# A spectral mixer with an MLP, forward and backward: order and engines in the opening stage

## The chip, the cores and the metric

The kernel runs on one core of a Trainium2 chip, in one launch. The metric is the device time of a run in microseconds (us). The core's engines, as the profile names them: PE (TensorE, matrix products; PEld are its weight loads), DVE (VectorE), ACT (ScalarE), POOL (GpSimd) and SP (SyncE, which only issues transfers here). Each works through its own instruction list in order and waits on semaphores for the others. Transfers are issued from SP's queue and from POOL's, and run on the same 16 DMA engines.

## The reference

The program computes a forward pass and all its gradients, for x of 2048 positions and 448 channels (S = 2048, D = 448), in bfloat16:

```
h  = x + irfft2(rfft2(layernorm(x)) * (w_r + i w_i))        # 2048 x 225 spectral weights
h2 = h + mlp(layernorm(layernorm(h)))                       # over positions: w1 2048x1792, gelu, w2 1792x2048
out, vjp = jax.vjp(h2, x, w_r, w_i, w1, b1, w2, b2);  grads = vjp(grad_out)
```

There are eight outputs: h2 and the gradients of the seven inputs. The gradient before the gelu needs w2 transposed times grad_out, which depends on no other stage: it is used as filler.

## The kernel before

Everything stays in SBUF where it can. Positions are cut into 16 rows h of 128 partitions. The stages, in order of time:

1. **Opening.** x comes in four quarters of four rows (`ld_x`). `Norm.stats` (L712) makes the statistics of a row on DVE (L717, L719); after the fourth row of a quarter `close` (L723) computes the root on ACT (L727) and the factors `rn` on DVE (L730, L732), and `make` (L774) or, for the first quarter, `make_mirrored` (L757) writes the *normal forms* `xln`: x scaled and shifted, on ACT (L777) or DVE (L780), whichever the planner picks from `self.alts`.
2. **Row transform** (`fft_rows`, L791). The first quarter goes straight to PE. For the others DVE *folds* the forms (two `u`, four `w`, L806, and a small copy, L525); then PE multiplies `w` with the table `kf`, and the result is copied from PSUM to `zt`.
3. **Column transform** (`fft_cols`, L830): PE products with `df` and, after additions on DVE (`gg`, L853), with `hf`, giving the spectrum `xs`. It starts when all of `zt` is there.
4. **Spectral product** (`cmul`, L887): DVE multiplies `xs` with the weights `w_t` (`t_r` and `t_i`, L896; results written into `w_t`, L903 and L905), in five groups of columns. The first `t_r` reads the weights as a whole, so it waits for all of `w_t`.
5. **Inverse transform** (`ifft_cols`, `ifft_rows`): products with `hi`, `di0`, `kinv`; DVE makes `eo` (L977, L979) and h (L1064), then statistics, and POOL writes the normal forms `hln` of h.
6. **Filler.** w2 transposed times grad_out (`ps_mg<-go_n,w2T`): 14 blocks of 16 products. A block needs its turned weights `w2T[j]`. Blocks 0 and 1 are loaded plain and turned on PE (`turn`, L603: 16 products with the identity in two halves, each copied out of PSUM by ACT or DVE, L612); the others are loaded by transposing transfers, which occupy SP's queue while they are set up.
7. **First layer** (`ps_mp<-hln,w1c`), gelu and its derivative on ACT and DVE (L1128 to L1148), second layer (`ps_mp<-gT,w2c`), and the backward stages: `ps_mm<-du,w1T` with the layernorm's gradient (`norm_back`), the transforms again, and the weight gradients.

**What sets the order.** The kernel only records operations (`Plan.op`): which engines can do each, with estimated costs, what it reads and writes, and a priority level `pl.boost`. `Plan.order` (L257) then places them one by one: the engine and the operation that can start first by the estimates; of those that can start at the same time, the one with the highest level plus remaining path. The result is a fixed instruction list for each engine. So a changed cost, level or alternative moves instructions on all engines. Transfers on SP have a fixed sequence, that of their `ld` calls (`place`); in the planner one server with a rate in bytes per us stands for the DMA engines.

**What the change touches.** The loads of the spectral weights, `ld_w` (L622): four transfers of 450 KB, for the real and the imaginary part, each in a lower half (partitions 0 to 63) and an upper half, all on SP, between the turned blocks w2T(3) and w2T(4). The normal forms in `Norm.make` (L774). The turning of the two plain blocks of w2 (L1030) and the loop over x's quarters (L1039), where `pl.boost` is 60 for the first quarter's statistics and 0 for the others.

Of the kernel before, what the change touches and what calls it, by code (L numbers as in the profile page):

```python
# [18 lines left out]
P = 128  # L19
S = 2048  # L20
D = 448
DF = 225
# [3 lines left out]
NJ = 16  # L26
# [395 lines left out]
def kernel(  # L422
# [40 lines left out]
    pl = Plan(nc, tc, rings)  # L463

    def const(name, shape, dtype=BF16):
        ring(name, 1)
        return pl.buf(name, shape, name, dtype)
# [10 lines left out]
    def big(i, shape, name, dtype=BF16):  # L478
        return pl.buf(f"X{i}", shape, name, dtype)
# [85 lines left out]
    x = big(0, [P, NT, D], "x")  # L565
# [37 lines left out]
    def turn(j, w2n):  # L603
        for a in range(0, NT, 8):
            pt = bank(sp[0], [P, 8, P], BF16)

            def go(e, on, a=a, pt=pt):
                for t in range(8):
                    e.transpose(pt[:, t], w2n[:, (a + t) * P:(a + t + 1) * P], ident[:])

            pl.op(mm(*[128] * 8), go, r=[(w2n, a), ident], w=[pt])
            copy(on_act(1024) + [("DVE", 0.62, 0.70)], lambda a=a: w2T[j][:, a:a + 8, :], lambda pt=pt: pt[:], [pt], [(w2T[j], a)])  # L612
            turned.append(pl.ops[-1])
# [5 lines left out]
        ld(t, lambda b: b[:], hnd[name].ap(), int(np.prod(shape)) * 2)  # L619
        return t  # L620

    def ld_w(dst):  # L622
        for c, src in enumerate((A_w_r, A_w_i)):
            v = src.rearrange("(q b r) k -> b q r k", b=2, r=NJ)
            for b_ in range(2):
                ld_parts(dst, [(c, b_)], lambda b, c=c, b_=b_: b[64 * b_:64 * b_ + 64, c], v[b_], 64 * NJ * DF * 2,
                         rate=0.225)

    ld_x(0)
    kf = const("kf", [P, 5, P])  # L630
# [13 lines left out]
    ld_w2T(2)  # L644
    ld_w2T(3)
    w_t = big(4, [P, 2, NJ, DF], "w_t")
    ld_w(w_t)
    ld_w2T(4)
    kinv = table("kinv", "kinv", [P, 3, P])
    di0 = table("di0", "di", [P, 2, 2, DC])  # L650
# [14 lines left out]
    def ld_w1(slot, j0, j1):  # L665
# [3 lines left out]
        for a in range(j0, j1, 2):  # L669
# [12 lines left out]
          w=[warm])  # L682
# [20 lines left out]
    class Norm:  # L703
# [6 lines left out]
        alts = [("DVE", 0.305, 0.39), ("ACT", 0.65, 0.76)]  # L710
# [63 lines left out]
        def make(self, dst, h):  # L774
            def go(e, on):
                if on == "ACT":
                    e.activation(out=dst[:, h, 0:D], in_=self.src[:, h, :], func=ACT.Identity,  # L777
                                 scale=self.rn[:, h, 0:1], bias=self.rn[:, h, 1:2])
                else:
                    e.tensor_scalar(out=dst[:, h, 0:D], in0=self.src[:, h, :], scalar1=self.rn[:, h, 0:1],  # L780
                                    scalar2=self.rn[:, h, 1:2], op0=ALU.mult, op1=ALU.add)

            pl.op(self.alts, go, r=[(self.src, h), (self.rn, (h, 0)), (self.rn, (h, 1))], w=[(dst, h)])

        def factors(self):

# [241 lines left out]

    xln = big(1, [P, NT, 450], "xln")
    for j in w2n:  # L1030
        turn(j, w2n[j])
    pl.boost = 60.0
    for k, sign in ((1, 1.0), (2, -1.0), (3, -1.0), (4, 1.0)):
        pl.op(on_act(128), lambda e, on, k=k, sign=sign: e.activation(
            out=kf[:, k, :], in_=kf[:, 0, :], func=ACT.Copy, scale=sign), r=[(kf, 0)], w=[(kf, k)])
# [2 lines left out]
    zt = big(2, [DC, 4, 32, 64], "zt")  # L1038
    for g in range(4):  # L1039
        for h in range(4 * g, 4 * g + 4):  # L1040
            pl.boost = 60.0 if g == 0 else 0.0
            nx.stats(h)
        pl.boost = 0.0
        if g == 0:
            for o in turned[:2]:
                o.soft.add(nx.root.idx)
        fft_rows(xln, zt, g, g == 0)
    xs = big(3, [P, 2, NJ, DF], "xs")
    fft_cols(zt, df1, xs)
    negate(hi, lambda: hi[:, :, 0, :], lambda: hi[:, :, 2, :], 1024, [(hi, 0)], [(hi, 1)])  # L1050
# [9 lines left out]
    for h in range(NT):  # L1060
        with grouped():
# [3 lines left out]
                out=hn[:, h, :], in0=py[:], in1=hn[:, h, :], scale=1.0, scalar=0.0, op0=ALU.add, op1=ALU.add,  # L1065
# [16 lines left out]
    for src, dst, n in ((b1r, b1c, NFB), (b2r, b2c, NT)):  # L1082
        pb = bank("mg", [P, n], BF16)
        pl.op(mm(128), lambda e, on, pb=pb, src=src, n=n: e.transpose(pb[:], src[:], ident[0:n, 0:n]),
              r=[src, ident], w=[pb])
        copy([("DVE", 0.1, 0.2)], lambda dst=dst: dst[:], lambda pb=pb: pb[:], [pb], [dst])
    pl.op(small(), lambda e, on: e.tensor_scalar(out=b1q[:], in0=b1c[:], scalar1=Q6, scalar2=None, op0=ALU.mult),
          r=[b1c], w=[b1q])
# [27 lines left out]
    for j in range(NFB):  # L1116
# [7 lines left out]
        def gop(alts, r, w, fn, ge=ge):  # L1124
# [4 lines left out]
            out=g(uf), in_=pu[:, 0:D], func=ACT.Identity, bias=b1c[:, j:j + 1]))  # L1129
        gop([("ACT", 0.516, 0.62)], [pu, b1q], [q_], lambda e, g, j=j, pu=pu: e.activation(  # L1130
            out=g(q_), in_=pu[:, 0:D], func=ACT.Square, bias=b1q[:, j:j + 1], scale=Q6))
# [88 lines left out]
    for t in range(NT):  # L1220
# [5 lines left out]
            r=[p2, b2c, hr[t // 2]], w=[h2])  # L1226
# [254 lines left out]
```

## Time and profile before

| what | value |
|---|---|
| three runs | 335.44, 336.0, 336.9 us; median 336.0 |
| the profiled execution | 335.88 us; its span 334.1 us; mean granted clock of TensorE 0.995 |
| transfers | 81.01 MB, mean 242 GB/s over the span |
| spectral weights w_t from SP (before the first spectral product) | two of w_r and two of w_i, 450 KB each |

How to read it: the span goes from the first to the last instruction; the run's time also holds what lies around it. A timeline row gives the start, the length, the engine, the line and operation, output and inputs, how many instructions the row merges, and in brackets how long the engine was idle before and what ended that. A row of the windows view gives the stretch, its length, the busy time and the count of PE, PEld, DVE, ACT and POOL, then PE's granted clock, the share of the DMA engines and GB/s. A row of the transfers' list gives destination and source, the queue, how many, KB of each and the median time from issue to landing. Matmuls are pipelined and their ends are modelled, so rows of PE overlap by a little.

### The profile page before, as it was taken

Reading aid. Unit: us, or ns where it says so; the run is one execution under the profiler, and the core shown is the slowest. Engines: PE = TensorE matmul, PEld = TensorE weight load, DVE = VectorE, ACT = ScalarE, POOL = GpSimd, SP = SyncE. Lnnn points to the kernel's source line nnn. Section 1 sums busy time; section 2 is a strip of 40 time slices with the busy share of each in tenths; the row PEclk is TensorE's granted clock in tenths of the full one; section 3 lists DMA queues with packets and bytes.
Section 4 is the critical chain, followed back from the end, with each engine's and each line's share of the span. In section 5 each row is a group of like instructions: output and inputs, shape, how many; then the busy total and the mean of one; then the engine's idle time right before and its main releaser. Section 6 shows DMA issues by size and latency. Waiting matters only on the chain.

```text
span 334.1 us, 7003 instructions
## 1 busy us (share of the span) xinstructions
PE 323.8 (97%) x2554; PEld 176.2 (53%) x2554; DVE 267.7 (80%) x762; ACT 207.1 (62%) x459; POOL 56.3 (17%) x98
## 2 busy tenths in 40 slices
PE   8969999999999999999999999999999999999994
PEld 2547755666655555555555555555555554454441
DVE  5997999898839999062157887797989799999994
ACT  3886744376668766082302222398887788988883
POOL 0000000036440111040232000000001114455100
PEclk9979999999999999999999999999999999999999
DMA  7999899998699999999989999999995326766656
GB/s 243 379 225 230 176 211 229 239 238 242 203 325 275 334 336 253 304 272 359 260 190 228 244 215 219 240 252 186 259 269 218 125 112 231 272 205 232 237 211 221
DMA packets 136319, 81.01 MB, mean 242 GB/s; under 512 B 94396, under 2 KB 128572, under 8 KB 136156
## 3 DMA queue, kind: packets, MB, share of 16 engines
q1 hardware_dynamic: 130620, 60.45, 77.1%
q0 software_dynamic: 5664, 20.10, 16.7%
q8 instruction: 20, 0.33, 0.4%
q14 instruction: 15, 0.12, 0.1%
HBM read 30.98 MB, written 27.08 MB: 174 GB/s over the span
## 4 chain that ended last, share of the span: by engine, by line
PE 70%; DVE 23%; ACT 3%; issue 2%; DMA 1%; DVEq 0%; ACTq 0%
PE ps_mp L536 25%; PE ps_mm L536 17%; PE ps_mg L536 10%; PE ps_sp L536 6%; PE ps_sb L536 5%; DVE junk L1262 4%; DVE junk L1285 3%; DVE bs_x L717 3%; PE ps_mw L536 3%; PE ps_mm L540 2%; ACT v L1267 2%; DVE gg L853 2%; DVE u L806 1%; DVE w L806 1%; DVE go_r L1288 1%
## 5 line engine op out<-in xcount | busy, mean ns | idle before, releaser
L523 ACT CAST s<-ps_mm 128x512 bf16<-128x512 f32 (+1 forms) x108 | 56.3, 580 | 6.2 <-PE ps_mm L536 5.4
L536 PE MATMUL ps_mm<-du,w1T 128*128 128x449 bf16 x224 | 43.4, 353 | 0.0
L536 PE MATMUL ps_mp<-hln,w1c 128*128 128x448 bf16 x224 | 42.9, 352 | 0.0
L536 PE MATMUL ps_mp<-gT,w2c 128*128 128x448 bf16 x224 | 42.9, 352 | 0.0
L536 PE MATMUL ps_mm<-goT,g_t 128*128 128x512 bf16 (+1 forms) x191 | 41.0, 380 | 0.0
L536 PE MATMUL ps_mg<-go_n,w2T 128*128 128x448 bf16 x180 | 39.9, 359 | 0.0
L536 PE MATMUL ps_mm<-du_t,hlnT 128*128 128x448 bf16 (+1 forms) x208 | 39.2, 353 | 0.0
L1267 ACT ACTIVATE v<-ps_mm,nm,rn_h 128x448 f32<-128x448 f32 x16 | 11.6, 724 | 43.0 <-DVE nm L1280 43.0
L536 PEld LDWEIGHTS <-w1T 128*128 128x128 bf16 x224 | 21.7, 97 | 21.0
L536 PEld LDWEIGHTS <-w2c 128*128 128x128 bf16 x224 | 21.9, 98 | 20.5
L536 PEld LDWEIGHTS <-w1c 128*128 128x128 bf16 x224 | 21.9, 98 | 20.3
L536 PEld LDWEIGHTS <-hlnT 128*128 128x128 bf16 (+1 forms) x256 | 19.3, 97 | 21.3 <-issue 7.0
L1224 DVE SCALAR_TENSOR_TENSOR h<-ps_mp,b2c,hr 128x448 bf16<-128x448 f32 x16 | 9.8, 677 | 16.7 <-PE ps_mp L536 16.7
L536 PEld LDWEIGHTS <-w2T 128*128 128x128 bf16 x180 | 16.2, 99 | 12.7 <-issue 1.5
L536 PEld LDWEIGHTS <-g_t 128*128 128x128 bf16 (+1 forms) x191 | 13.2, 96 | 17.1 <-issue 6.0
L1132 DVE SCALAR_TENSOR_TENSOR ge<-ge 128x448 bf16<-128x448 bf16 x14 | 8.7, 621 | 13.4 <-ACT ge L1130 13.4
L1128 ACT ACTIVATE ge<-ps_mp,b1c 128x448 bf16<-128x448 f32 x14 | 8.8, 626 | 14.1 <-PE ps_mp L536 12.8
L1262 DVE CUSTOM_DVE_ANT_0 junk<-v,hln 128x448 bf16<-128x448 f32 x16 | 10.0, 623 | 7.8 <-ACT v L1267 7.7
L515 POOL DMA_DIRECT2D hn_d<-x x4 | 2.4, 588 | 75.0 <-DVE rn_h L732 71.2
L536 PEld LDWEIGHTS <-kinv 128*128 128x128 bf16 x144 | 11.3, 98 | 6.7 <-DVE eo L979 2.5
L1267 ACT ACTIVATE v<-y,nm,rn_x 128x448 f32<-128x448 f32 x16 | 12.3, 771 | 3.8 <-DVE nm L1274 3.8
L1231 ACT ACTIVATE gb2j<-go_r 128x448 bf16<-128x448 bf16 x16 | 9.2, 574 | 7.6 <-DMA go_r<-in_grad_out_dram 7.2
(157 smaller groups left out, 629.1 us busy)
## 6 DMA issues: line engine op xcount, KB each, us to landing
w2c<-in_B_w_dram SPq DMA_DIRECT2D x8, 896.0 KB, 9.1
w1c<-in_B_w_dram SPq DMA_DIRECT2D x6, 1024.0 KB, 11.2
out_dram<-s POOLq DMA_DIRECT2D x8, 512.0 KB, 3.0
out_dram<-s POOLq DMA_DIRECT2D x8, 448.0 KB, 3.4
out_dram<-s SPq DMA_DIRECT2D x7, 448.0 KB, 2.6
out_dram<-s SPq DMA_DIRECT2D x6, 512.0 KB, 5.2
x<-in_A_x_dram SPq DMA_DIRECT2D x4, 448.0 KB, 6.6
go_n<-in_grad_out_dram SPq DMA_DIRECT2D x2, 896.0 KB, 10.3
```

Source lines behind the costliest of these rows:

```text
L523: e.copy(out=out(), in_=in_())
L536: e.matmul(out, lhsT=lhsT, rhs=rhs(), start=start, stop=stop)
L540: e.matmul(out[a:b_], lhsT=lhsT[:, a // each:b_ // each], rhs=rhs(), start=start, stop=stop)
L717: pl.op(on_dve(448, 1.0e-3, 0.07), lambda e, on: e.bn_stats(out=bs[:], in_=self.src[:, h, :]), r=[(self.src, h)], w=[bs])
L806: pl.op(tt(4 * n), lambda e, on: e.tensor_tensor(out=out(), in0=in0(), in1=in1(), op=op), r=r, w=w_)
L1128: gop([("ACT", 0.516, 0.62)], [pu, b1c], [uf], lambda e, g, j=j, pu=pu: e.activation(out=g(uf), in_=pu[:, 0:D], func=ACT.Identity, bias=b1 ...
L1132: gop(stt, [q_, uf], [zz], lambda e, g: e.scalar_tensor_tensor(out=g(zz), in0=g(q_), scalar=6.0 * GELU_C, in1=g(uf), op0=ALU.add, op1=ALU. ...
L1224: pl.op([("DVE", 0.595, 0.68)], lambda e, on, t=t, p2=p2, h2=h2: e.scalar_tensor_tensor(out=h2[:], in0=p2[:, 0:D], scalar=b2c[:, t:t + 1], ...
L1231: pl.op([("ACT", 0.70, 0.80)], lambda e, on, h=h: e.activation(out=gb2j[:], in_=go_r[:, h, :], func=ACT.Copy, accum_out=gb2[:, h:h + 1]), ...
L1262: pl.op([("DVE", 0.605, 0.73)], lambda e, on: e.tensor_tensor_reduce(out=junk[:], in0=src(), in1=xhat(), scale=scale(), scalar=0.0, op0=AL ...
L1267: pl.op([("ACT", 0.53, 0.64)], lambda e, on: e.activation(out=v[:], in_=rowsum(), func=ACT.Identity, scale=nm.rn[:, h, 0:1], bias=ab[:, 1:2]),
L1285: pl.op([("DVE", 0.595, 0.68)], lambda e, on: e.scalar_tensor_tensor(out=junk[:], in0=xhat(), scalar=by(), in1=v[:], op0=ALU.mult, op1=ALU ...
```

## The change

Five edits:

- In the turning of w2's two plain blocks, the second block gets level 100.
- The statistics of x's second quarter get level 50.
- The normal forms of x's third and fourth quarters may be made by POOL too.
- The first use of `ld_w` loads only the lower halves on SP, with another rate in the planner's estimate.
- The upper halves are loaded by a new function, `ld_w_upper`, from POOL's queue. Its first operation copies one column of the last normal form (`xln` of row 15) to `mark`, and the two transfers read `mark`, so they are issued behind it.

```diff
-    def ld_w(dst):
+    def w_rows(src):
+        return src.rearrange("(q b r) k -> b q r k", b=2, r=NJ)
+
+    def ld_w_upper(dst, gate, key):
+        mark = const("mark", [P, 1])
+        pl.op([("POOL", 0.1, 0.2)], lambda e, on: e.tensor_copy(out=mark[:], in_=gate()), r=[key], w=[mark])
         for c, src in enumerate((A_w_r, A_w_i)):
-            v = src.rearrange("(q b r) k -> b q r k", b=2, r=NJ)
-            for b_ in range(2):
+            def go(e, on, c=c, src=src):
+                e.dma_start(out=dst[64:128, c], in_=w_rows(src)[1])
+            pl.op([("POOL", 0.6, 0.6)], go, r=[mark], w=[(dst, (c, 1))], dma=(64 * NJ * DF * 2, 0.335e6, False))
+
+    def ld_w(dst, halves=2):
+        for c, src in enumerate((A_w_r, A_w_i)):
+            v = w_rows(src)
+            for b_ in range(halves):
                 ld_parts(dst, [(c, b_)], lambda b, c=c, b_=b_: b[64 * b_:64 * b_ + 64, c], v[b_], 64 * NJ * DF * 2,
-                         rate=0.225)
+                         rate=0.225 if halves == 2 else 0.335)
...
-    ld_w(w_t)
+    ld_w(w_t, 1)
...
-            pl.op(self.alts, go, r=[(self.src, h), (self.rn, (h, 0)), (self.rn, (h, 1))], w=[(dst, h)])
+            alts = self.alts + [("POOL", 0.72, 0.78)] if self.nm == "x" and h // 4 in (2,3,) else self.alts
+            pl.op(alts, go, r=[(self.src, h), (self.rn, (h, 0)), (self.rn, (h, 1))], w=[(dst, h)])
...
     for j in w2n:
+        pl.boost = 100.0 if j else 0.0
         turn(j, w2n[j])
...
-            pl.boost = 60.0 if g == 0 else 0.0
+            pl.boost = (60,50,0,0)[g]
             nx.stats(h)
...
         fft_rows(xln, zt, g, g == 0)
+    ld_w_upper(w_t, lambda: xln[:, 15, 0:1], (xln, 15))
     xs = big(3, [P, 2, NJ, DF], "xs")
```

In the instruction lists of the changed program, the opening differs so:

- PE: the 16 products of block 1 stand right behind the turning of it, ahead of the fold products of x's second quarter; 50 block products, not 38, stand ahead of the first column product. The two small turns of the biases (L1084) and the fifth block come earlier among the column products.
- ACT: three normal forms behind the first quarter's, not eight, and one copy of the second turned block, not two; that copy stands behind one `du` eviction.
- DVE: three forms of the second quarter, not one, then the statistics of the third and the fourth quarter with the two `u` folds of the second between them, then the third quarter's factors, the other copy of the turned block, three forms, and the remaining folds. The first `t_r` stands behind 12 `gg` additions and one eviction, where it was 18 and two.
- POOL: three normal forms, the copy to `mark` and two transfers of `w_t`, all ahead of its work of before.
- SP: two transfers fewer, the rest in the order of before.
- From about 180 us on, the lists of all engines are the same but for a few neighbours exchanged on DVE.

## The prediction

> **What bounds the kernel now.** I read the page first (busy shares, then the clock by slices), then the timeline of TensorE, then those of the engines that end its waits.
>
> ```profile
> span 334.1 us, 7003 instructions
> ...
> PE 323.8 (97%) x2554; PEld 176.2 (53%) x2554; DVE 267.7 (80%) x762; ACT 207.1 (62%) x459; POOL 56.3 (17%) x98
> ...
> GB/s 243 379 225 230 176 211 229 239 238 242 203 325 275 334 336 253 304 272 359 260 190 228 244 215 219 240 252 186 259 269 218 125 112 231 272 205 232 237 211 221
> ```
>
> TensorE is busy for 323.8 of 334.1 us, so only 10.3 us of idle time can be had there. The profiled execution took 335.88 us, 1.8 us more than its span and 0.1 us under the median of 336.0. I make the sum against 335.88. The timeline shows where the idle time is (start, length, instructions, and in brackets the idle time before):
>
> ```profile
> 13.74 3.19 PE L536 MATMUL ps_mg<-go_n,w2T 128*128 128x448 bf16 x16
> 17.10 1.07 PE L609 MATMUL ps_sp<-ident,w2n 128*128 128x128 bf16 x16 [0.17 <-DMA w2n<-in_B_w_dram]
> 20.89 1.90 PE L536 MATMUL ps_sp<-kf,w 128*113 128x128 bf16 x16 [2.72 <-DVE w L525]
> 22.58 3.72 PE L536 MATMUL ps_mg<-go_n,w2T 128*128 128x448 bf16 x14
> ...
> 27.03 0.54 PE L536 MATMUL ps_mg<-go_n,w2T 128*128 128x448 bf16 x2
> ...
> 28.30 1.30 PE L536 MATMUL ps_mg<-go_n,w2T 128*128 128x448 bf16 x6
> 29.53 1.23 PE L536 MATMUL ps_sp<-df,zt 113*64 113x113 bf16 x40
> ```
>
> The large hole is 2.72 us, ended by VectorE's fold of x's second quarter. What follows it is slow as well:
>
> ```profile
> 20.00:22.00 2.00, 1.11 (x11) 1.11 (x12) 2.00 (x10) 2.00 (x4) 0.00 (x0) 0.75 1.39 170
> 22.00:24.00 2.00, 2.00 (x12) 1.19 (x11) 1.50 (x5) 2.00 (x5) 0.00 (x0) 0.50 1.73 228
> ```
>
> The third column from the right is the granted clock: 0.75, then 0.50. The 14 block products from 22.58 take 3.72 us, where 14/16 of the row at 13.74 are 2.79; the 16 fold products take 1.90 us, where the 16 turns of the same 128 columns at 17.10 take 1.07. So hole and clock cost 2.7 + 0.9 + 0.8 = 4.4 us. Later products take 0.19 us each (37.62 us for 198, quoted below). From here to the end TensorE hardly waits, so what is won here is kept only if nothing else holds it up later.
>
> **The change part by part.** Order and counts of the changed program are from its instruction order; the durations are from rows here.
>
> *W2's second turned block first.* Its two copies stand last on ScalarE:
>
> ```profile
> 19.51 1.90 ACT L523 COPY w2T<-ps_sp 128x1024 bf16<-128x1024 bf16 x2
> ```
>
> They wait behind four normal forms, though the turned block is there at 18.17 (17.10 + 1.07). In the changed order ScalarE makes only three forms after the first quarter, not eight, and its copy stands right behind the du eviction. So it can start near 17.7 and end 0.95 later, at 18.7; VectorE copies the other half. TensorE's order puts that block's 16 products (16 x 0.19 = 3.05 us) ahead of the second quarter's fold, to 21.8. This is the filling of the hole.
>
> *Statistics ahead, and who makes the forms.* VectorE pays for it:
>
> ```profile
> 10.52 0.66 DVE L525 COPY w2T<-ps_sp 128x1024 bf16<-128x1024 bf16 x1
> ...
> 12.28 2.20 DVE L717 BATCH_NORM_STATS2 bs_x<-x 128x6 f32<-128x448 bf16 x4
> ...
> 20.63 0.21 DVE L525 COPY w<-u 128x16 bf16<-128x16 bf16 x1
> 20.76 1.01 DVE L780 TENSOR_SCALAR xln<-x,rn_x 128x448 bf16<-128x448 bf16 x3
> ...
> 22.88 1.16 DVE L806 TENSOR_TENSOR u<-xln 128x896 bf16<-128x896 bf16 x2 [0.50 <-ACT zt L523]
> ...
> 26.01 0.19 DVE L525 COPY w<-u 128x16 bf16<-128x16 bf16 x1
> ```
>
> A form costs 0.31 us (1.01 for three, whose ends overlap the next), a block copy 0.6. Ahead of the second quarter's last fold copy (20.63 to 20.84) now stand two more forms of that quarter (0.62), one block copy (0.6) and three later forms that came behind it (0.93): 23.0 instead of 20.84. All four folds end two forms and a copy later, less the 0.50 us wait at 22.88, which goes: 26.2 + 0.62 + 0.6 - 0.5 = 26.9. So VectorE's part alone is a loss of 0.7 us.
>
> *GpSimd's three forms.* No row of before has GpSimd at work in this stretch. It makes such forms later:
>
> ```profile
> 72.42 2.94 POOL L780 TENSOR_SCALAR hln<-x,rn_h 128x448 bf16<-128x448 bf16 x4
> ```
>
> That is 0.73 us each, 2.2 for three. They can start when VectorE has written the third quarter's factors, which its new order puts behind both sets of statistics and the first two folds: 12.3 (its first statistics of before) + 0.6 for two forms + 2 x 2.4 + 1.1 = 18.8. So they end at 21.0, before VectorE needs them. But they touch VectorE:
>
> ```profile
> 73.35 0.50 DVE L732 SCALAR_TENSOR_TENSOR rn_h<-mv_h,rn_h 128x2 f32<-128x2 f32 x1
> ...
> 78.26 0.16 DVE L732 SCALAR_TENSOR_TENSOR rn_h<-mv_h,rn_h 128x2 f32<-128x2 f32 x1
> ...
> 80.08 0.22 DVE L732 SCALAR_TENSOR_TENSOR rn_h<-mv_h,rn_h 128x2 f32<-128x2 f32 x1
> ```
>
> The same small instruction with two SBUF operands takes 0.16 us, but 0.50 inside GpSimd's run: it ends at 73.85, where GpSimd's second form ends (72.42 + 2 x 0.73 = 73.88). So VectorE can be held until GpSimd is done. The folds have two SBUF operands each, and GpSimd's three forms now lie beside two of them, the factors and three forms of VectorE's own. The hold lies between 0 and 2.2 us (all three forms, one after the other); I take 1.0, as the block copy, which reads PSUM, runs in the meantime. The folded data are then there at 24.0 for the second quarter and at 27.9 for the fourth; for the third 1.4 earlier than that, at 26.5 (behind it come only four short folds, about as long as the two at 22.88, and a copy).
>
> TensorE then: fold products at 24.0 (0.9), 8 block products (1.5), fold at 26.5 (0.9), 4 products (0.8), fold at 28.2 (0.9), and the column products 1.23 us behind, as 29.53 stands behind 28.30: 30.3. That is 0.8 us later than 29.53, but 50 block products are done by then, not 38 (16 + 14 + 2 + 6): 12 x 0.19 = 2.3 us. **Ahead by 1.5 us.** The hole is now 0.5 + 2.2 us in two pieces; I reckon with the full clock, since TensorE works for 3 us between them.
>
> *The upper halves on GpSimd's queue.* The rows of SP and of the transfers (KB each, us from issue to landing):
>
> ```profile
> 22.53 1.93 SPq L583 DMA_DIRECT2D w_t<-in_A_w_r_dram  x2
> 24.50 1.24 SPq L583 DMA_DIRECT2D w_t<-in_A_w_i_dram  x2
> 25.91 8.29 SPq L509 DMA_TRANSPOSE w2T<-in_B_w_dram  x1
> ```
> ```profile
> w_t<-in_A_w_r_dram SPq DMA_DIRECT2D x1, 450.0 KB, 5.8
> ```
> ```profile
> w_t<-in_A_w_i_dram SPq DMA_DIRECT2D x1, 450.0 KB, 9.5
> ```
> ```profile
> w2T<-in_B_w_dram SPq DMA_TRANSPOSE x1, 11.9
> ```
>
> The first half lands at 28.3, the last (issued at 25.1) at 34.6: 2.1 us for each 450 KB. The turned block behind them lands at 37.8. On GpSimd the two issues follow its forms, near 22 to 23.5, when SP issues the other two, and nothing behind them on that queue is due before some 70 us (the row at 72.42 is among its first work). Who needs it sooner now: block products 65 and on (fifth block) come behind 88 column products (40 take 1.23 us), 14 block products and 16 small ones in the changed order, some 5.6 us after the columns start: 35.9; and the first spectral product on VectorE:
>
> ```profile
> 30.35 3.12 DVE L853 TENSOR_TENSOR gg<-ps_sp,gb 128x226 bf16<-128x226 f32 x10 [1.23 <-ACT gb L523]
> 33.38 1.14 DVE L525 CAST xs<-ps_sp 128x450 bf16<-128x450 f32 x2
> ...
> 36.86 1.08 DVE L896 TENSOR_TENSOR t_r<-xs,w_t 128x1800 bf16<-128x1800 bf16 x1
> ```
>
> It stands behind 12 gg and one eviction instead of 18 and two: 36.86 + 0.8 - 6 x 0.31 - 0.5 = 35.3. If halves on two queues run beside each other, the four take between 4.2 us and 8.4; I take 5.5, so that all is there by 32 and the fifth block by 35. Then neither waits.
>
> [...]
>
> *From 30 to 95 us.* VectorE is all but full, so TensorE's lead must fit it.
>
> ```profile
> 40.71 0.38 PE L536 MATMUL ps_sp<-gg,hf 128*64 128x225 bf16 x4 [0.36 <-DVE gg L853]
> ...
> 87.55 2.43 PE L536 MATMUL ps_mp<-hln,w1c 128*128 128x448 bf16 x12
> 89.82 0.56 PE L536 MATMUL ps_sp<-eo,kinv 128*128 128x225 bf16 x6
> 90.22 37.62 PE L536 MATMUL ps_mp<-hln,w1c 128*128 128x448 bf16 x198
> ```
> ```profile
> 81.52 0.62 DVE L525 CAST du<-ps_mg 128x448 bf16<-128x448 f32 x1 [1.22 <-PE ps_mg L536]
> ...
> 89.33 0.38 DVE L979 TENSOR_TENSOR eo<-ps_sp,odd 128x224 bf16<-128x224 f32 x1
> ```
> ```profile
> 93.30 1.41 POOL L780 TENSOR_SCALAR hln<-x,rn_h 128x448 bf16<-128x448 bf16 x2
> ```
>
> The wait at 40.71 goes: 1.85 ahead. The last inverse-row products end at 90.22 with 12 first-layer products done; in the changed order 18 are. By TensorE's work they end at 90.22 + 6 x 0.19 - 1.85 = 89.5. By VectorE: its part at 89.7 comes 0.8 later, less the 1.22 us that it waited for TensorE at 81.52: 89.3 plus 0.4 for the products. They meet near 89.5 to 89.7. Then 28 first-layer products (5.3 us) stand ahead of the first that needs the last two rows, now 24. Those rows were ready 4.5 us after 90.22 (93.30 + 1.41 = 94.71), so at 94.1, in time for 94.9. Before it was 94.8 with 36 products done; now 46 are. **10 x 0.19 - 0.1 = 1.8 us.**
>
> *The rest.* The GELU stage has room:
>
> ```profile
> 143.06 0.62 DVE L1132 SCALAR_TENSOR_TENSOR ge<-ge 128x448 bf16<-128x448 bf16 x1 [9.65 <-ACT ge L1130]
> ```
>
> VectorE stands idle for 9.65 us before its last column, so a TensorE that is early finds the others done. From 180 us on all engines keep the order of before; the 1.8 us are carried: **335.88 - 1.8 = 334.1 us.** With a hold of 0 the lead is 2.8 (333.1), with 2.2 it is 0.7 (335.2).
>
> **The rivals.**
> - *The transfers gain nothing.* The halves share one limit, the fifth block lands at 37.8, due at 35.9: TensorE waits 1.9 us and the lead is gone, 336.0. For it: the share of the DMA engines is 1.39 and 1.73 in the rows of 20 to 24 us; against it: 170 and 228 GB/s is less than the early slices' 379.
> - *GpSimd blocks VectorE in full, and the clock falls again.* The hold is 2.2, the second quarter comes at 25.2, a hole of 3.4 us opens behind 21.8, longer than the 2.72 that halved the clock, and 1.7 us are lost: 0.7 - 1.7 = 1.0 slower, 336.9, or half of it where later waits hide some: 336.4. The row at 73.35 speaks for it; PSUM copies between speak against a full hold. [...]
> - *VectorE waits for GpSimd's transfers (slower).* Place: the first spectral product, L896, due at 35.3. VectorE works in order, so the gg of all later columns wait behind it, and through them TensorE. In the forecast both engines meet at 89.5, so what VectorE loses here isn't given back. If GpSimd's queue is served only behind SP's (fifth block at 37.8), its halves come 4.2 us later, at 42; half way between due and that is 39: 334.1 + 3.7 = 337.8. It decides from 35.3 + 1.8 = 37.1, where the gain is gone, and is slower than before from there. Against it: its two issues come beside SP's, not behind.
> - *More is won.* No hold, and neither engine waits up to 95 us: of the 4.4 only the 0.5 us before the block products and VectorE's 0.7 are lost: 335.88 - 3.2 = 332.7.
>
> **How the numbers follow.** Forecast 0.58 (own range 333.1 to 335.2), transfers 0.10, block and clock 0.08, late halves 0.16, more 0.08. A measurement of this kernel can tell about 0.5%, 1.7 us, from no change. The forecast is faster by more than that (under 334.3) in 0.47 and within it in 0.11; with "more", 0.55 faster. Same: 0.11 + 0.10 + 0.05 of the block = 0.26. Slower: 0.16 + 0.03 = 0.19. The range is 332.6 to 336.6: it leaves out the late halves and little else.
>
> **What would show it.** Right: 16 block products between the turns and the second quarter's fold, no slice under 0.9 in the clock after 17 us, columns near 30.3, no wait of TensorE for a turned block near 36, L896 without a wait for a transfer, and the last rows' first-layer products near 95. Wrong: fold instructions of 0.5 us or more beside GpSimd's forms, a clock of 0.5 near 25, or an idle VectorE ahead of L896.

## The result and the profile after

The changed kernel is slower: 339.54, 340.26 and 340.38 us, beside 335.44, 336.0, 336.32 and 336.9 for the kernel before on the same chip; ratio 1.0116 (95%: 1.0083 to 1.0148), 3.9 us. Every ratio leaves out the executions that took over 1.5% more than the fastest of the same kernel, here one of 349.21 us at a mean clock of 0.973. The profiled execution took 340.38 us, before 335.88: 4.5 us more. The forecast was 334.1, its range ended at 336.6.

The page of the kernel after, then the chain of waits of both pages, before first:

```profile
span 338.6 us, 6994 instructions
...
PE 323.8 (96%) x2539; PEld 174.4 (52%) x2550; DVE 267.3 (79%) x764; ACT 203.4 (60%) x454; POOL 60.5 (18%) x104
```
```profile
PE 70%; DVE 23%; ACT 3%; issue 2%; DMA 1%; DVEq 0%; ACTq 0%
```
```profile
PE 64%; DVE 17%; DMA 10%; ACT 3%; SPq 2%; issue 2%; DVEq 0%; ACTq 0%
```

TensorE is busy for the same 323.8 us in a span 4.5 us longer: on the whole its work became no dearer, TensorE waits more. And the chain that ends last now runs through transfers for 10% of the span, 1% before. The timeline of TensorE shows which (start, length, ..., in brackets the idle time before and what ended it). Lines are numbered as in each kernel: L745, L793, L820, L867 and L910 of the kernel after are L732, L780, L806, L853 and L896 of before.

```profile
17.39 1.07 PE L609 MATMUL ps_sp<-ident,w2n 128*128 128x128 bf16 x16 [0.24 <-DMA w2n<-in_B_w_dram]
19.12 3.20 PE L536 MATMUL ps_mg<-go_n,w2T 128*128 128x448 bf16 x16 [0.66 <-ACT w2T L523]
23.86 1.10 PE L536 MATMUL ps_sp<-kf,w 128*113 128x128 bf16 x16 [1.54 <-DVE w L525]
...
28.29 0.55 PE L536 MATMUL ps_mg<-go_n,w2T 128*128 128x448 bf16 x2 [0.38 <-DMA w2T<-in_B_w_dram]
...
30.80 1.22 PE L536 MATMUL ps_sp<-df,zt 113*64 113x113 bf16 x40
...
37.68 0.57 PE L540 MATMUL ps_mg<-go_n,w2T 128*64 128x448 bf16 x4 [0.97 <-DMA w2T<-in_B_w_dram]
...
48.08 1.70 PE L540 MATMUL ps_mg<-go_n,w2T 128*64 128x448 bf16 x8 [2.37 <-DMA w2T<-in_B_w_dram]
...
55.64 1.11 PE L536 MATMUL ps_sp<-hi,w_t 64*113 64x128 bf16 x32
...
94.68 0.96 PE L536 MATMUL ps_sp<-eo,kinv 128*128 128x225 bf16 x12
```

Up to 30.8 it goes nearly as forecast: the 16 products fill the hole, which is now 0.66 + 1.54 us instead of 2.72. But TensorE, which before waited for no turned block, waits for three: 0.38 us for w2T(3), 0.97 for the fifth block w2T(4), and 2.37 for the seventh, w2T(6). (A row L540 x8 is four products, each in two halves of 64 columns.) Behind the last gap the clock falls, in the windows view (third column from the right):

```profile
46.00:48.00 2.00, 0.00 (x0) 0.00 (x0) 2.00 (x6) 0.29 (x1) 0.00 (x0) 1.00 1.09 111
48.00:50.00 2.00, 1.92 (x9) 0.67 (x10) 2.00 (x5) 0.00 (x0) 0.00 (x0) 0.53 0.95 215
50.00:52.00 2.00, 2.00 (x14) 0.83 (x12) 1.56 (x5) 0.53 (x1) 0.00 (x0) 0.62 1.22 245
```

The `gg,hf` products stand behind the waiting block in TensorE's list, so ScalarE and VectorE run dry: ScalarE stands idle for 4.91 us ahead of 51.20, VectorE for 3.77 us ahead of 55.33 (its row is below). The `hi` products begin at 55.64, before at 49.70, with 114 block products done, not 102. The last inverse rows end at 95.48, before at 90.22, with 18 first-layer products done, not 12: 5.26 - 6 x 0.19 = 4.1 us behind, and nothing later gives it back.

Why the blocks were late: issues and landings of the transfers of the kernel after (KB each, us from issue to landing; the two rows of w2T are w2T(4), issued at 24.73, and w2T(6), issued at 39.73).

```profile
22.52 0.71 POOL L631 DMA_DIRECT2D w_t<-in_A_w_r_dram  x1
23.23 0.55 POOL L631 DMA_DIRECT2D w_t<-in_A_w_i_dram  x1
```
```profile
23.33 0.60 SPq L583 DMA_DIRECT2D w_t<-in_A_w_r_dram  x1
23.97 0.58 SPq L583 DMA_DIRECT2D w_t<-in_A_w_i_dram  x1
24.73 9.29 SPq L509 DMA_TRANSPOSE w2T<-in_B_w_dram  x1
...
39.73 4.71 SPq L509 DMA_TRANSPOSE w2T<-in_B_w_dram  x1
```
```profile
w_t<-in_A_w_r_dram POOLq DMA_DIRECT2D x1, 450.0 KB, 5.4
w_t<-in_A_w_i_dram POOLq DMA_DIRECT2D x1, 450.0 KB, 7.0
w_t<-in_A_w_r_dram SPq DMA_DIRECT2D x1, 450.0 KB, 9.0
w_t<-in_A_w_i_dram SPq DMA_DIRECT2D x1, 450.0 KB, 10.5
```
```profile
w2T<-in_B_w_dram SPq DMA_TRANSPOSE x1, 12.9
```
```profile
w2T<-in_B_w_dram SPq DMA_TRANSPOSE x1, 8.3
```

In the kernel before, w2T(6) reads:

```profile
39.34 4.53 SPq L509 DMA_TRANSPOSE w2T<-in_B_w_dram  x1
```
```profile
w2T<-in_B_w_dram SPq DMA_TRANSPOSE x1, 6.8
```

The four halves land at 27.9, 30.2, 32.3 and 34.5: one behind the other, 2.1 to 2.3 us apart, as on one queue (2.1, last at 34.6). On two queues the last half landed 0.1 us sooner. So w2T(4) lands at 24.73 + 12.9 = 37.6 (before 37.8) and w2T(6) at 48.0 (before 39.34 + 6.8 = 46.1).

But the planner had been told 0.335 for a half (460,800 bytes at 335,000 bytes per us: 1.38 us), not 0.225 (2.05 us, near the 2.1 to 2.3 of the landings). For four halves that is 2.7 us, so it took every later turned block for 2.7 us earlier, and put its products earlier into TensorE's fixed list. Before, TensorE came to the first product of w2T(6) at 48.08, 2 us behind its landing:

```profile
48.08 0.92 PE L540 MATMUL ps_mg<-go_n,w2T 128*64 128x448 bf16 x8
```

After, it came there at 45.71, 2.4 us sooner, and had to wait until the very same 48.08. The earlier place is one half of that wait. The other is that the block landed 1.9 us later than before: it was under way for 8.3 us, not 6.8. With the landing of before, the wait would have been 0.4 us; with the place of before, there would have been none. Why it took longer isn't shown; with the same lists on one queue (e17) it took 8.3 us too.

### The profile page after: what moved, and what is told of

It is laid out like the page before. It is cut to its first block, busy times and chain, and to the rows that moved or that the text cites. A ratio compares the mean times of both kernels' runs of the same rounds, so it can differ in the third digit from the quotient of the medians.

```text
span 338.6 us, 6994 instructions
## 1 busy us (share of the span) xinstructions
PE 323.8 (96%) x2539; PEld 174.4 (52%) x2550; DVE 267.3 (79%) x764; ACT 203.4 (60%) x454; POOL 60.5 (18%) x104
## 4 chain that ended last, share of the span: by engine, by line
PE 64%; DVE 17%; DMA 10%; ACT 3%; SPq 2%; issue 2%; DVEq 0%; ACTq 0%
PE ps_mp L536 25%; PE ps_mm L536 15%; PE ps_mg L536 8%; DMA w2T<-in_B_w_dram 8%; PE ps_sb L536 5%; PE ps_sp L536 5%; DVE junk L1278 4%; DVE junk L1301 4%; DMA w2n<-in_B_w_dram 3%; PE ps_mw L536 2%; PE ps_mm L540 2%; ACT v L1283 2%; SPq L583 2%; PE ps_mg L540 2%; DVE go_r L1304 1%
## 5 line engine op out<-in xcount | busy, mean ns | idle before, releaser
L536 PE MATMUL ps_mp<-hln,w1c 128*128 128x448 bf16 x224 | 43.3, 352 | 0.0
L536 PE MATMUL ps_mm<-du,w1T 128*128 128x449 bf16 x224 | 43.3, 353 | 0.0
L536 PE MATMUL ps_mp<-gT,w2c 128*128 128x448 bf16 x224 | 42.7, 352 | 0.0
L536 PE MATMUL ps_mg<-go_n,w2T 128*128 128x448 bf16 x184 | 41.0, 355 | 1.0 <-ACT w2T L523 0.7
L536 PE MATMUL ps_mm<-goT,g_t 128*128 128x512 bf16 (+1 forms) x180 | 40.0, 380 | 0.9 <-issue 0.5
L536 PE MATMUL ps_mm<-du_t,hlnT 128*128 128x448 bf16 (+1 forms) x208 | 39.2, 353 | 0.0
L1283 ACT ACTIVATE v<-ps_mm,nm,rn_h 128x448 f32<-128x448 f32 x16 | 11.6, 723 | 42.1 <-DVE nm L1296 42.1
L536 PEld LDWEIGHTS <-w1T 128*128 128x128 bf16 x224 | 21.7, 97 | 21.0
L536 PEld LDWEIGHTS <-w2c 128*128 128x128 bf16 x224 | 21.9, 98 | 20.5
L536 PEld LDWEIGHTS <-w1c 128*128 128x128 bf16 x224 | 21.7, 98 | 19.7
L536 PEld LDWEIGHTS <-hlnT 128*128 128x128 bf16 (+1 forms) x256 | 19.3, 97 | 21.3 <-issue 7.0
L536 PEld LDWEIGHTS <-w2T 128*128 128x128 bf16 x184 | 15.9, 98 | 14.8 <-issue 1.8
L536 PEld LDWEIGHTS <-g_t 128*128 128x128 bf16 (+1 forms) x191 | 13.3, 97 | 17.0 <-issue 6.0
L536 PEld LDWEIGHTS <-kinv 128*128 128x128 bf16 x144 | 11.5, 98 | 6.8 <-DVE eo L993 2.3
L540 PE MATMUL ps_mg<-go_n,w2T 128*64 128x448 bf16 x80 | 11.1, 384 | 3.3 <-DMA w2T<-in_B_w_dram 3.3
L867 DVE TENSOR_TENSOR gg<-ps_sp,gb 128x226 bf16<-128x226 f32 x30 | 10.4, 410 | 4.8 <-ACT gb L523 4.8
```

What stands on the lines that cost most here:

```text
L536: e.matmul(out, lhsT=lhsT, rhs=rhs(), start=start, stop=stop)
L540: e.matmul(out[a:b_], lhsT=lhsT[:, a // each:b_ // each], rhs=rhs(), start=start, stop=stop)
L867: pl.op(on_dve(226), lambda e, on, s_=s_, op=op: e.tensor_tensor(out=g_[:, s_, :].rearrange("p (k t) -> p t k", t=2), in0=pr[:, 0:2, :], i ...
L1283: pl.op([("ACT", 0.53, 0.64)], lambda e, on: e.activation(out=v[:], in_=rowsum(), func=ACT.Identity, scale=nm.rn[:, h, 0:1], bias=ab[:, 1:2]),
```

## The experiments

Ratios are to the kernel before on the same chip, with their 95% interval. A first theory (A: the wrong rate) stood against two rivals (B: the opening's edits cost it by themselves; C: the second queue slows the transposing loads). A2, from e5 on, adds to A that GpSimd's transfers hold up w2T(3). Theory S, from e9 on, joins A and part of B: turned blocks are a stock, and who uses them sooner lacks them later.

**e1**, the changed kernel with the old rate:

```diff
-                         rate=0.225 if halves == 2 else 0.335)
+                         rate=0.225)
...
-            pl.op([("POOL", 0.6, 0.6)], go, r=[mark], w=[(dst, (c, 1))], dma=(64 * NJ * DF * 2, 0.335e6, False))
+            pl.op([("POOL", 0.6, 0.6)], go, r=[mark], w=[(dst, (c, 1))], dma=(64 * NJ * DF * 2, 0.225e6, False))
```

> Four edits as in the changed kernel, two queues as there, but the planner is given the old rate (225 KB/us, 0.225) for all four w_t transfers. Theory A (the estimate): the changed kernel's loss comes from the planner's faster rate for the halves, by which it put the products of turned blocks w2T(4) and w2T(6) into TensorE's list 2.7 us sooner while the transfers landed no sooner. Then this kernel has no wait of TensorE above 1 us for a turned block between 36 and 50 us and takes 335 to 337 us. Theory B (the opening): the forms on GpSimd, the statistics ahead and the second turned block first cost it by themselves (columns start 1.3 us later). Then 339 to 341 us. Theory C (the second queue): transfers on GpSimd's queue beside SP's slow SP's transposing ones. Then 339 to 341 us.

Ten runs from 336.49 to 343.23, median 341.28; the ratio, of the five up to 340.94, is 1.0070 (1.0029 to 1.0111). Theory A alone misses it. The profiled execution was the fastest (336.49): w2T(3) landed 6.3 us after its issue, and TensorE waited only 0.96 us, for w2T(4).

**e2.** The kernel that ran under this label had e1's loads by mistake, so what was expected below wasn't tried here (e5 does). It is a second run of e1.

> The changed kernel with all four w_t transfers on SP as before (old rate): the lists of the compute engines are those of e1, only the queue of the upper halves differs. Theory A: within 1 us of e1, 335 to 337 us, and the fifth turned block lands within 0.5 us of e1's. Theory B: 339 to 341 us. Theory C: 335 to 337 us, and 3 us or more under e1.

340.1 to 342.8; ratio 1.0157 (1.0106 to 1.0209). Its profile, an execution of 342.01, shows what e1's of 336.49 lacks (its lines are numbered four higher, so L540 here is L536 elsewhere, a product in one piece):

```profile
31.31 0.55 PE L540 MATMUL ps_mg<-go_n,w2T 128*128 128x448 bf16 x2 [3.53 <-DMA w2T<-in_B_w_dram]
```

w2T(3) landed 10.9 us after its issue, not 6.3 (7.8 in the changed kernel). GpSimd's halves are issued while it is still under way, and the changed order wants it at 27.8, where the order before wanted it at 33.45.

**e3**, the kernel before with one number changed, the planner's rate:

```diff
-                         rate=0.225)
+                         rate=0.335)
```

> The kernel before with one number changed: the planner's rate for the four w_t transfers is 0.335 instead of 0.225. No transfer, queue or engine alternative changes; only the order of the lists follows. Theory A: 338 to 340 us, TensorE waits 2 us or more for a turned block between 40 and 50 us, since the planner starts w2T(6) at 42.9 by its own clock instead of 45.8. Theories B and C: 335.5 to 336.8 us, as before.

339.7 us, ratio 1.0101 (1.0059 to 1.0142): no transfer changed, and 3.4 us are lost. TensorE's timeline:

```profile
38.97 2.44 PE L536 MATMUL ps_mg<-go_n,w2T 128*128 128x448 bf16 x12 [2.18 <-DMA w2T<-in_B_w_dram]
...
49.41 3.58 PE L536 MATMUL ps_mg<-go_n,w2T 128*128 128x448 bf16 x18 [1.86 <-DVE gg L853]
```

The wait stands at w2T(4), not at w2T(6), as this order differs. The rate alone does harm.

**e4**, the kernel before with two queues and the old rate: of the change only the loads, and e1's two lines.

```diff
-    ld_w(w_t)
+    ld_w(w_t, 1)
...
+    ld_w_upper(w_t, lambda: xln[:, 15, 0:1], (xln, 15))
```

> The kernel before with only the upper halves of w_t on GpSimd's queue and the old rate in the planner: the lists of PE, VectorE and ScalarE are those of before. Theory A: 335.5 to 337 us, last half landed within 1 us of before's 34.6. Theory B: the same. Theory C: 339 to 341 us.

336.24 us, ratio 0.9997 (0.9966 to 1.0027). With the lists of before the second queue wins nothing, and in nine of ten executions it costs nothing: C falls as the cause of the loss. The tenth, left out of the ratio, took 347.03; it is the profiled one, and in it w2T(4) took 22.9 us and GpSimd's halves 18.3 and 21.0 (see the last section).

**e5**, the changed kernel with one queue and the old rate:

```diff
-    ld_w(w_t, 1)
+    ld_w(w_t)
...
-    ld_w_upper(w_t, lambda: xln[:, 15, 0:1], (xln, 15))
```

> The changed kernel with all four w_t transfers on SP behind w2T(3), as before, and the old rate; the lists of PE, VectorE and ScalarE are those of e1. (The kernel that ran as e2 had e1's loads by mistake and is a second run of e1.) Theory A2: besides the planner's rate, the transfers on GpSimd's queue start while w2T(3) is still under way and hold it up (it landed 6.3, 7.8 and 10.9 us after its issue in e1, the changed kernel and e2), just where the changed order wants it. Then here w2T(3) lands within 6 us of its issue, TensorE doesn't wait for it, and the time is 335 to 337 us with a spread under 2 us. Theory B (the opening edits lose by themselves): 339 to 342 us, as e2.

337.83 to 339.52, ratio 1.0071 (1.0042 to 1.0099): 2.4 us lost by the opening, between the two expectations. The wait for w2T(3) is gone and the spread is 1.7 us, but:

```profile
38.39 0.93 PE L536 MATMUL ps_mg<-go_n,w2T 128*128 128x448 bf16 x4 [2.32 <-DMA w2T<-in_B_w_dram]
```

TensorE stands for 2.32 us ahead of the fifth block, and for 0.71 ahead of a later one at 50.10. The hole of 2.72 us at 18 us has moved to 36.

**e6, e7, e8**: e5 without GpSimd's forms; the kernel before with GpSimd's forms alone; e5 with 1.5 us added to the planner's landing of each turned block. The three edits (e6 on e5, e7 on the kernel before, e8 on e5):

```diff
-            alts = self.alts + [("POOL", 0.72, 0.78)] if self.nm == "x" and h // 4 in (2,3,) else self.alts
-            pl.op(alts, go, r=[(self.src, h), (self.rn, (h, 0)), (self.rn, (h, 1))], w=[(dst, h)])
+            pl.op(self.alts, go, r=[(self.src, h), (self.rn, (h, 0)), (self.rn, (h, 1))], w=[(dst, h)])
```
```diff
-            pl.op(self.alts, go, r=[(self.src, h), (self.rn, (h, 0)), (self.rn, (h, 1))], w=[(dst, h)])
+            alts = self.alts + [("POOL", 0.72, 0.78)] if self.nm == "x" and h // 4 in (2,3,) else self.alts
+            pl.op(alts, go, r=[(self.src, h), (self.rn, (h, 0)), (self.rn, (h, 1))], w=[(dst, h)])
```
```diff
-                o.end = server + 1.1
+                o.end = server + 1.1 + (1.5 if turned else 0.0)
```

> As e5, but GpSimd makes no normal forms: only the second turned block first and x's second statistics ahead are left of the change. Theory A2: 335.5 to 337.5 us (columns 0.5 to 1 us later than in e5, as three more forms stand on VectorE and ScalarE). Theory B with GpSimd's hold on VectorE as the cost: 1 us or more under e5.

339.49 us, ratio 1.0101 (1.0070 to 1.0132): TensorE waits 2.49 us for w2T(4) and 1.08 for a later block. Without GpSimd's forms it is no faster, so they aren't what costs.

> The kernel before with one edit: the normal forms of x's third and fourth quarters may be made by GpSimd. Theory A2: 335 to 337 us, columns within 0.7 us of before's 29.5. Theory B with the hold as the cost: 337.5 to 339 us.

336.89 us, ratio 1.0012 (0.9994 to 1.0031). The columns start at 28.02, 1.5 us sooner than before, and nothing comes of it: TensorE then waits 0.78 and 0.75 us for turned blocks.

> As e5, and the planner takes each turned block to land 1.5 us later than by its rate, so that its products are placed later. Theory A2: 334.5 to 336.5 us and no wait of TensorE over 0.5 us for a turned block. Theory B: as e5.

339.1 us, ratio 1.0072 (1.0044 to 1.0099). In its trace, of the slowest of five executions (341.43), no wait for a turned block is left, but TensorE waits for VectorE's folds not once (1.58 us, as in e5) but twice (1.58 and 1.47), the products from 26.77 on take longer (16 fold products 1.96 us, in e5 1.10; four block products 1.70, in e5 0.92), and the columns start at 33.5, in e5 at 30.16: without blocks to work on the time is lost elsewhere.

**e9, e10, e11** shorten what lies ahead of the blocks without touching a list: the imaginary weights' two transfers are left out of the changed kernel (e9), of e5 (e10) and of the kernel before (e11), while the planner is told the old sizes. GpSimd fills one column of the part that isn't loaded, and the outputs are not the reference's.

```diff
+            if skip:
+                return
             kw = {"transpose": True} if transpose else {}
             e.dma_start(out=out(dst), in_=in_() if callable(in_) else in_, **kw)
...
-                out=t[:], in0=a[:, :, j0:j1, :], in1=b[:, c:c + 1, j0:j1, :].broadcast_to([P, 2, n, DF]),
+                out=t[:], in0=a[:, :, j0:j1, :], in1=b[:, c * conj:c * conj + 1, j0:j1, :].broadcast_to([P, 2, n, DF]),
```

> The changed kernel with the two transfers of the imaginary spectral weights left out (one on each queue, 900 KB); the first spectral product uses the real part twice instead, so the spectrum is not the reference's. The planner is told the old sizes, so the lists of PE, VectorE and ScalarE are those of the changed kernel. Theory S (the stock): until w2T(4) lands TensorE has only four turned blocks, 64 products; the changed opening spends 16 of them in the hole at 18 to 21 us and so stands without work ahead of w2T(4) instead, and the wrong rate adds the wait for w2T(6). With 900 KB less ahead of it, w2T(4) lands near 33.5, no wait for a turned block over 0.7 us is left behind 32 us, and the time is 333.5 to 335.5 us. Theory B (the opening loses by itself, whatever lands when): 338 to 340 us.

335.73 us, ratio 0.9974 (0.9946 to 1.0001): 4.8 us less than the changed kernel (1.0116 - 0.9974 = 1.42%), with its very lists. TensorE's timeline has no wait for a turned block left but the first:

```profile
28.01 0.55 PE L536 MATMUL ps_mg<-go_n,w2T 128*128 128x448 bf16 x2 [0.85 <-DMA w2T<-in_B_w_dram]
...
50.21 1.11 PE L536 MATMUL ps_sp<-hi,w_t 64*113 64x128 bf16 x32
...
89.27 0.96 PE L536 MATMUL ps_sp<-eo,kinv 128*128 128x225 bf16 x12
```

w2T(4) lands at 31.3 and w2T(6) at 42.1. The last inverse rows end at 90.07, before at 90.22, with 18 first-layer products done, not 12: 0.15 + 6 x 0.19 = 1.3 us ahead, where 1.8 were forecast. This is near the forecast's course, on transfers that the change didn't bring. The time shows 0.9 us of it, with an interval that reaches no change.

> The same left out of the kernel before, as the control. Theories S and B: 335.3 to 336.8 us, since before doesn't wait for a turned block. If less traffic is worth something by itself: under 335 us.

336.48 us, ratio 1.0003 (0.9978 to 1.0027). The control: with the order of before, less traffic is worth nothing that can be told.

> The same left out of e5 (one queue, old rate, lists of e5). Theory S: the wait of 2.3 us ahead of w2T(4) goes, 334.5 to 336.3 us, about 2.5 under e5. Theory B: 337.5 to 339 us.

338.1 us, ratio 1.0024 (0.9990 to 1.0058), 1.6 us under e5 and not 2.5. The wait for w2T(4) is gone; TensorE waits 1.22 us for VectorE at 41.45 instead. Its profiled execution began late (w2's first plain block landed 1.3 us later than in e5, TensorE waited 2.59 us for it); whether the others did, no trace tells.

**e12**, e5 with w2T(4) loaded ahead of all of w_t:

```diff
+    ld_w2T(4)
     w_t = big(4, [P, 2, NJ, DF], "w_t")
     ld_w(w_t)
-    ld_w2T(4)
```

> As e5, with w2T(4) loaded ahead of the four w_t transfers, not behind them; the planner knows it. Theory S: w2T(4) lands by 31 us and TensorE doesn't wait for it; the first spectral product waits for w_t instead (lands 2 to 3 us later, 37 to 38 us), so 335.5 to 337.5 us. Theory B: 338 to 340 us.

339.28 us, ratio 1.0065 (1.0032 to 1.0097). The wait for w2T(4) goes, and one of 1.69 us for a later block (48.27) and one of 1.74 at 69.97 come. The first spectral product was expected to wait for the weights and doesn't: among VectorE's waits from 17 to 96 us none is for a transfer. The planner made new lists here, so e12 doesn't tell the transfers' part from that of the lists.

**e13**, e1 with GpSimd's transfers gated by w2T(3) in place of the last normal form:

```diff
-    ld_w_upper(w_t, lambda: xln[:, 15, 0:1], (xln, 15))
+    ld_w_upper(w_t, lambda: w2T[3][:, 0, 0:1], w2T[3])
```

> As e1 (two queues, old rate), but GpSimd's two transfers wait for w2T(3) to land, not for the last normal form. Theory A2 (they hold up w2T(3)): w2T(3) lands 5 to 6.5 us after its issue, TensorE waits under 0.5 us for it, and the runs lie within 2.5 us of each other, at 336 to 339 us. Rival (scatter comes from the start of the kernel): runs spread over 4 us or more as in e1, median 340 or more.

338.69 to 346.11; ratio, of the two up to 343.32, 1.0138 (1.0051 to 1.0225). In the trace, of an execution of 346.02 us, w2T(3) lands after 5.7 us and isn't waited for, as expected; the time isn't as expected. There w2T(4) is issued beside GpSimd's transfers and takes 18.8 us:

```profile
43.61 1.71 PE L540 MATMUL ps_mg<-go_n,w2T 128*64 128x448 bf16 x8 [8.56 <-DMA w2T<-in_B_w_dram]
```
```profile
w_t<-in_A_w_r_dram POOLq DMA_DIRECT2D x1, 450.0 KB, 13.9
w_t<-in_A_w_i_dram POOLq DMA_DIRECT2D x1, 450.0 KB, 15.5
```

**e14, e15, e16** load w2T(4) between the real and the imaginary weights, with the first `t_r` waiting for the real part alone: on e5, on e5 without the statistics' level, and on the kernel before. `ld_w` gets an argument `cs` for the parts to load.

```diff
-    ld_w(w_t)
-    ld_w2T(4)
+    ld_w(w_t, cs=(0,))
+    ld_w2T(4)
+    ld_w(w_t, cs=(1,))
...
-                op=ALU.mult), r=ra + rb, w=[t])
+                op=ALU.mult), r=ra + ([(b, (0, 0)), (b, (0, 1))] if rb == [b] and not c and j0 == 6 else rb), w=[t])
```

> As e5, with w2T(4) loaded between the real and the imaginary weights; the first t_r waits for the real part alone, t_i for both. All data are loaded. Theory S: w2T(4) lands by 34, the wait ahead of it (2.3 us in e5) goes, t_i waits at most 1 us: 335 to 337 us, and the time from the second turning of w2 to the end is 316 to 317.5 us (e5 319.1, before 317.0). Theory B: 338 to 340 us.

337.43 us, ratio 1.0037 (1.0012 to 1.0062). w2T(4) lands 7.5 us after its issue and isn't waited for; by the medians half of e5's loss is back, though the two intervals overlap. From the second turning of w2 to the end the trace takes 316.3 us, as theory S expected (e5 319.1, before 317.0). But TensorE came to that turning only at 21.42, in e5 at 17.27, and a late TensorE finds the blocks further on.

> As e14 without the level for the second quarter's statistics: the second turned block first and GpSimd's forms are left. If the statistics ahead cost VectorE time (columns at 30.2 in e5, 28.0 in e7): 0.5 to 1.5 us under e14. If they are what fills VectorE: the same or slower.

337.6 us, ratio 1.0033 (1.0007 to 1.0059): the statistics' level makes no difference that can be told.

> The kernel before with only the place of w2T(4) changed as in e14. Theory S: before doesn't wait for w2T(4), so nothing is won: 335.5 to 337.5 us. If an earlier fifth block were worth something by itself: under 335.3 us.

336.29 us, ratio 0.9991 (0.9958 to 1.0025): nothing, as expected.

**e17**, the lists of the changed kernel (its wrong rate kept) with one queue; on e5:

```diff
-                         rate=0.225 if halves == 2 else 0.335)
+                         rate=0.335 if dst.name == "w_t" else 0.225)
```

> The lists of PE, VectorE and ScalarE are those of the changed kernel (its wrong rate kept), but all four w_t transfers stand on SP. Theory S with the wrong rate as the second cause: w2T(4) and w2T(6) land where they did in the changed kernel within 1 us, TensorE waits for both, 3 to 5 us in all, and the time is 339 to 341 us: the second queue is worth nothing and costs nothing on the whole here. If the second queue is what costs: 336 to 338.5 us.

339.84 us, ratio 1.0118 (1.0072 to 1.0165), as the changed kernel's 1.0116, with the same two waits:

```profile
38.47 0.57 PE L540 MATMUL ps_mg<-go_n,w2T 128*64 128x448 bf16 x4 [1.35 <-DMA w2T<-in_B_w_dram]
...
48.41 0.95 PE L540 MATMUL ps_mg<-go_n,w2T 128*64 128x448 bf16 x8 [1.93 <-DMA w2T<-in_B_w_dram]
```

The loss is in the lists; the second queue has no part in it that can be told.

**e18**, GpSimd's forms alone with w2T(4) between the weights (e7's edit and e14's on the kernel before):

> The kernel before with GpSimd's forms for the third and fourth quarter and w2T(4) between the real and the imaginary weights (columns early by e7, fifth block early by e16). Theory S: nothing of it lies ahead of a wait that sets the end, so 335.3 to 336.8 us. If the 1.5 us by which e7's columns start sooner count once the block is there: 334 to 335.2 us.

334.13 to 336.67, median 334.85; ratio 0.9978 (0.9955 to 1.0000): 0.7 us faster than before, at the border of what can be told, and the second of the two expectations. Columns start at 27.8, the `hi` products at 47.7 (before 49.70), and TensorE waits for a turned block once, 0.52 us.

## Why the prediction was wrong

**What bounds the kernel: right for the stage, incomplete as a bound.** The hole of 2.72 us and the low clock were there. But the forecast took the block products that fill it as free. They are a stock: until w2T(4) lands near 37.7, TensorE has four blocks, 64 products, and the kernel before ended the last of them at 38.3, just in time. Whoever spends 16 of them at 19 us lacks them at 36. e5 shows it (2.32 us ahead of w2T(4)), e9 and e11 that it goes when the block comes early and that only the changed order gains by it.

**The opening: right, but for the 0.38 us that TensorE waited for w2T(3).** Forecast and trace after: second block's products up to 21.8 (22.3), fold of the second quarter 24.0 (23.86), columns 30.3 (30.80) with 50 products done, the clock at 1.00 in every window of 2 us from 14 to 40. The hold by GpSimd (VectorE waiting while GpSimd works) was taken as 1.0 us, between 0 and 2.2. VectorE's rows beside GpSimd's forms, then its first spectral product and its longest idle time:

```profile
20.32 0.52 DVE L745 SCALAR_TENSOR_TENSOR rn_x<-mv_x,rn_x 128x4 f32<-128x4 f32 x1
20.76 0.39 DVE L820 TENSOR_TENSOR w<-u 128x448 bf16<-128x448 bf16 x1
21.07 0.93 DVE L793 TENSOR_SCALAR xln<-x,rn_x 128x448 bf16<-128x448 bf16 x2
...
35.80 1.08 DVE L910 TENSOR_TENSOR t_r<-xs,w_t 128x1800 bf16<-128x1800 bf16 x1
...
55.33 0.72 DVE L867 TENSOR_TENSOR gg<-ps_sp,gb 128x226 bf16<-128x226 f32 x2 [3.77 <-ACT gb L523]
```
```profile
19.25 2.62 POOL L793 TENSOR_SCALAR xln<-x,rn_x 128x448 bf16<-128x448 bf16 x3 [18.80 <-DVE rn_x L745]
```

The factors took 0.52 instead of 0.16, two forms 0.93 instead of 0.7 (three in 1.01 before), the folds nothing more (0.39): about 0.6 us of hold by these rows, and 0.87 us a form on GpSimd, not 0.73. The copy of the turned block out of PSUM, taken to run in the meantime, took 0.69 us beside GpSimd's forms (at 19.35), 0.66 without them (at 10.50).

**The step that failed** is "The upper halves on GpSimd's queue": "If halves on two queues run beside each other, the four take between 4.2 us and 8.4; I take 5.5, so that all is there by 32 and the fifth block by 35. Then neither waits." That they run beside each other was the author's estimate, and no run shows it. They land one after the other, 2.1 to 2.3 us each, the last at 34.5 and the fifth block at 37.6. It was due at 36.71 (35.9 forecast), so TensorE waited 0.97 us for it where the sum had nothing. VectorE didn't wait: `t_r` ran at 35.80 with all weights landed, so the rival that was to end slower had the wrong place.

**The rival that had the landing (the fifth block at 37.8, measured 37.6), "the transfers gain nothing", had the wrong price.** It gave 1.9 us for the fifth block alone and so 336.0. The wait there was 0.97. What it and the forecast left out is that the order was made with the wrong rate, so that every later block was due too soon as well. The terms by the trace: the lead at the columns is 12 x 0.19 - 1.27 = 1.0 us (30.80 against 29.53), with the 0.38 us for w2T(3) already in it; the waits behind that are 0.97 + 2.37 = 3.3; the three rows of block products from 48.08 take 1.70, 0.93 and 1.20 us instead of 0.95, 0.55 and 0.92 at full clock, 1.4 more. 1.0 - 3.3 - 1.4 = -3.7 us, of the -4.1 found at 95 us; 0.4 us isn't accounted for.

**How the loss divides.** Opening with the true rate and one queue: 2.4 us (e5). The wrong rate on top: 1.0118 - 1.0071, 1.6 us (e17), with intervals that overlap; by itself, on the order of before, it cost 3.4 (e3), so the parts don't simply add. The second queue: nothing in the comparison with the lists of before (e4) and of the changed kernel (e17), but it is a risk: with the true rate's lists the same program gave 1.0070 and 1.0157 (e1, e2), where one queue gave 1.0071 (e5). Opening and rate together are lost to blocks that land late: 4.8 us come back in e9. What stays open: with the true rate's lists an early fifth block brought back only 1.1 to 1.6 of the 2.4 us (e14, e10), with intervals that overlap e5's. From the second turning to the end, the traces of e10, e14 and e15 take 316.7, 316.3 and 316.4 us, no more than before's 317.0. But these executions came to that turning 2.4 to 4.2 us later than e5 did, so whether all of e5's loss is the stock's, or some of it lies elsewhere, wasn't settled.

**A second step failed with it, and cost more: "From 30 to 95 us"** has no term for the blocks behind w2T(4). The forecast followed two dates, w2T(4) and `t_r`. The wait for w2T(6) measured 2.37 us, and the low clock behind it 1.4 more. Its due date, 45.7, followed from the changed order, and the trace of before had its landing (issued at 39.34, landed at 46.1); the two weren't compared. That comparison alone would have given a wait of 0.4 us; the rest came with a landing 1.9 us later, which no row of before shows.

## What to carry to other kernels

Filler that is fed by transfers is a stock with delivery dates: filling a hole with it gains only if the next delivery comes sooner too, so compare the new due date of every later piece with its landing in the old trace, not only of the next one, and leave room for a landing that differs: w2T(6) took 6.8 us in one trace here and 8.3 in another. A planner's figure for a transfer is part of the program: a rate that is too high cost 3.4 us (e3) without changing a transfer. And spreading equal transfers over two queues didn't make them land sooner here: the last of four at 34.5 us, on one queue at 34.6.

## What the runs showed of the hardware

- A transposing transfer and plain ones from GpSimd's queue took far longer in two traces where GpSimd's were issued behind it. In the traced execution of e13, w2T(4) took 18.8 us and GpSimd's halves 13.9 and 15.5, when GpSimd's were issued 0.8 and 1.5 us behind w2T(4); in the profiled execution of e4, one of 347.03 us where the other nine took 335.5 to 338.8, 22.9, 18.3 and 21.0 (issued 1.0 and 1.7 us behind). Where GpSimd's were issued 2.2 and 1.5 us ahead of w2T(4), in the changed kernel, they took 5.4 and 7.0 and w2T(4) 12.9. The cause wasn't tried.
- The length of a gap alone didn't decide in these traces whether the clock fell behind it. It fell behind gaps of 2.37 us (to 0.53 and 0.62 in the windows from 48 to 52, the changed kernel) and 2.72 us (to 0.75 and 0.50 in those from 20 to 24, before), and stayed at 1.00 behind 2.32 us (e5) and 2.49 us (e6). In e8, behind two gaps of 1.58 and 1.47 us with 1.1 us of work between them, 16 fold products took 1.96 us, 1.10 behind the first gap alone. What decides it no run here shows.
